# Linear attention, Fourier mixing and a two-layer network in one kernel: the rectifier of the plain groups' second halves moves to one engine, and two pacing numbers behind the folds change

## The chip, the cores and the metric

The kernel runs on one core of a Trainium2 chip. The time is the device time of one execution in microseconds (us); the number that counts is the median of several executions. All arithmetic is in float32.

A core has five engines that run their own instruction queues beside each other: TensorE (PE in the profile) multiplies matrices and transposes, VectorE (DVE) and ScalarE (ACT) work element by element, GpSimd (POOL) does element-wise work and indirect transfers, SyncE (SP) issues most of the other transfers. Each engine takes its instructions in the order in which they stand in its queue, so an instruction that waits holds up all that stand behind it.

## The reference

```
# attention: B=4 batches, H=8 heads, S=768 positions, D=64, decay lam[h] per head
for each block b of 64 positions:
    intra = ((q_b @ k_b^T) * lam^(i-j) for i>=j) @ v_b
    out_b = intra + (q_b * lam^(pos+1)) @ state
    state = lam^64 * state + (k_b * lam^(63-pos))^T @ v_b
x = out, heads side by side                        # [4, 768, 512]
# Fourier mixing and the network
u  = x + real(fft(fft(x, over positions), over channels))
un = (u - mean(u)) / sqrt(var(u) + 1e-6)           # per position
result = u + max(un @ w_ch1, 0) @ w_ch2            # 512 -> 2048 -> 512
```

## The kernel before, in words

**Front and groups.** For each batch b a front runs: the attention (`attn`, six chunks of 128 positions, parts `attn_in` and `attn_out`) and then the Fourier mixing with the normalisation (`fft_ln`). The mixing uses symmetries: rows are added to and subtracted from their mirror images before the transform. These additions are the folds (`fold_a`, `fold_b`, helper `fold_x`), on VectorE. The mirrored rows are first written to DRAM (tiles `xa`, `xb`, by ScalarE's queue, lines 372 to 376) and then gathered back in reverse order by GpSimd (`mirror_a`, `mirror_b`, lines 448 to 461). After the folds come five DFT tiles over the positions (line 525), each copied out by ScalarE (line 529) into `ys`, and then for three tiles t in turn the DFT over the channels (`width`, lines 537 to 542), its combination on VectorE (lines 607 to 611) and the normalisation (`norm`, lines 554 to 585; the power of the variance is taken on GpSimd, line 559).

A batch gives three groups of 256 positions, and the twelve groups are put through the network in two ways. The first four, the list `PLAIN` (batch 0's three groups and batch 1's first), are multiplied directly by `mlp`. The other eight, `LATE`, go in pairs through a recursive product scheme with fewer multiplications (`late`), which needs sums of the weights that `combine_weights` makes on VectorE (line 709). `LATE[-1][0]` is the last batch, 3.

**A plain group.** `mlp(b, g, f0, f1)` takes the hidden channels f0 to f1 in tiles of 128. For each tile four products of 128x128 by 128x256 (line 644; the profile shows each as two instructions) fill a PSUM tile `pm`, of which there are three; the rectified tile goes into `hr`. Then the second layer (line 658) sums over the hidden tiles into PSUM and VectorE adds the result to u (lines 665, 666 or 669, 670). The first three plain groups are run in two calls, hidden tiles 0 to 7 and 8 to 15, the fourth in one call of 0 to 15. In a call that ends at the last hidden tile (`f1 == FO`, FO = 16), the odd tiles are rectified by VectorE (line 650) and the even ones by ScalarE (line 652); in the others all are rectified by ScalarE.

**What sets the order.** All these parts are Python generators. Each yields a number, its declared duration, after it has issued some instructions, and `weave` runs two of them beside each other by these numbers:

```
for d in lead:
    t_lead += d
    while t_other < t_lead * ratio:
        d = next(other, None)
        ...
        t_other += d
```

So the follower is advanced until its declared time has reached the leader's times `ratio`. In the stretch that matters the leader is `fr` (the rest of batch 2's front and batch 3's), the follower `back` (the second halves of the first three plain groups, then the fourth group), and the ratio is (t_back - t_half) / (t_rest - t_rest * t_half / t_back), which comes to t_back / t_rest = 167.6 / 193.6 = 0.8657. A plain step of one hidden tile declares 1.7, a chunk of four second-layer products over 512 columns declares 3.4. In `fft_ln`, lines 513 to 517, the folds of batches 1 to 3 are issued at once (`run`), and a number that is yielded after them makes room for plain work in front of the DFT.

The framework then orders each engine's queue once more: it keeps dependencies, estimates when an instruction could start, and may take a later one first. `keep_in_program_order` pins an instruction behind those that were issued before it; it is used on the first additions of a fold (lines 435, 436) and on the first DFT product of a batch (line 528).

When both fronts are done, the front's memory is released, the first input of the late groups (`ur`) is loaded by ScalarE's queue (`load_u(0, nc.scalar)`, lines 759 and 1233), the first six weight sums are woven with what is left of `back` (line 1234), the last two follow (line 1241), and `late` begins with the sums of line 792 to 798 and the products of line 891.

Of the kernel before, what the change touches and what calls it, by code (L numbers as in the profile page):

```python
# [15 lines left out]
AF = mybir.ActivationFunctionType  # L16
ALU = mybir.AluOpType
# [59 lines left out]
def kernel(  # L77
# [10 lines left out]
    nc = tc.nc  # L88
# [9 lines left out]
    FO = DFF // 128  # L98
# [40 lines left out]
    def new(pool, shape, tag, **kw):  # L139
        cnt[0] += 1  # L140
        return pool.tile(shape, F32, tag=tag, name=f"{tag}{cnt[0]}", **kw)

    def psum_a(shape):
        return new(pa, shape, "pa")

    def psum_m(shape):
        return new(pm, shape, "pm")
# [109 lines left out]
    LEADS = (0,)  # L257
# [207 lines left out]
    def fold_a(b):  # L465
        for a, n in enumerate(BLK):
            yield from fold_x(b, a, n, 1, eo[b][a][1][0:n, 1, 0:DM], xn_[b, HC + a][0:n])

    def fold_b(b, sets):

        tt = nc.vector.tensor_tensor
        for a, n in enumerate(BLK):
            yield from fold_x(b, a, n, 0, xs[b, a][0:n], xs[b, HC + a][0:n])
            e, o = eo[b][a]
            nc.scalar.copy(e[0:n, :, HM:HM + 1], e[0:n, :, DM - 1:DM])

            am, bm = e[0:n, :, W:2 * W], o[0:n, :, W:2 * W]
            lo, hi = e[0:n, 0, 0:HM + 1], e[0:n, 1, 0:HM + 1]
            tt(am[:, 0, 0:HM + 1], lo, hi, op=ALU.add)
            tt(am[:, 1, 0:HM + 1], lo, hi, op=ALU.subtract)  # L480
            yield 0.8

            lo, hi = am[:, :, 0:QM], am[:, :, HM:QM:-1]
            tt(e[0:n, :, 0:QM], lo, hi, op=ALU.add)
            tt(e[0:n, :, QM:HM], lo, hi, op=ALU.subtract)
            yield 0.8
            lo, hi = o[0:n, 0, 1:HM], o[0:n, 1, 1:HM]
            tt(bm[:, 0, 1:HM], lo, hi, op=ALU.subtract)
            tt(bm[:, 1, 1:HM], lo, hi, op=ALU.add)
            yield 0.8  # L490
            lo, hi = bm[:, :, 1:QM + 1], bm[:, :, HM - 1:QM - 1:-1]
            tt(o[0:n, :, 0:QM], lo, hi, op=ALU.subtract)
            tt(o[0:n, :, QM:HM], lo, hi, op=ALU.add)
            yield 0.8
            sets.append((e, o))
        eo.pop(b)
# [3 lines left out]
    def fft_ln(b):  # L500
# [7 lines left out]
        if b in LEADS:  # L508
            yield from fold_a(b)
            yield from fold_b(b, sets)  # L510
            yield 2.0
        else:
            yield 1.0
            run(fold_a(b))
            yield 6.0 if b - 1 in LEADS else 3.0
            run(fold_b(b, sets))
            yield 12.0 if b - 1 in LEADS else 9.0


        for i in range(5):  # L520
            ps = psum_a([128, 2, NK])
# [75 lines left out]
        for t in (1, 2, 0):  # L597
            ps = psum_a([128, DM])
# [14 lines left out]
            if t == 0:  # L613
                ps = psum_a([128, DM])
# [12 lines left out]
    PLAIN, LATE = ORDER[:4], ORDER[4:]  # L627

    def store(b, T, y, cols=slice(0, DM)):
        if T < HC:  # L630
            nc.sync.dma_start(out[b, 128 * T:128 * T + 128, cols], y[:, cols])
        else:
            nc.gpsimd.indirect_dma_start(out=out.rearrange("b s d -> (b s) d"),
                                         out_offset=row_of(2 + HC * (b + 1) + T - HC),
                                         in_=y[:, :], in_offset=None)

    def mlp(b, g, f0=0, f1=FO):

        ut = uts[b, g]
        hr = []  # L640
        for fc in range(f0, f1):
            ps = psum_m([128, G * 128])
            for c in range(KO):
                nc.tensor.matmul(ps, lhsT=w1[:, c, 128 * fc:128 * fc + 128], rhs=ut[:, c, :],  # L644
                                 start=(c == 0), stop=(c == KO - 1))
            if fc % 4 == 0:
                hr.append(new(hp_, [128, 4, G * 128], "hr"))
            t = hr[-1][:, fc % 4, :]
            if fc % 2 and f1 == FO:
                nc.vector.tensor_scalar(t, ps, 0.0, None, op0=ALU.max)  # L650
            else:
                nc.scalar.activation(t, ps, AF.Relu)  # L652
            yield 1.7
        for i in range(G):
            T = TT[g][i]
            ps = psum_m([128, DM])
            for fc in range(f0, f1):
                nc.tensor.matmul(ps, lhsT=hr[(fc - f0) // 4][:, fc % 4, 128 * i:128 * i + 128], rhs=w2[:, fc, :],  # L658
                                 start=(fc == f0), stop=(fc == f1 - 1))
                if fc % 4 == 3 and fc < f1 - 1:  # L660
                    yield 3.4
            u = xs[b, T]
            tt = nc.vector.tensor_tensor
            if f1 < FO:
                tt(u[:, 0:HM], ps[:, 0:HM], u[:, 0:HM], op=ALU.add)
                tt(u[:, HM:DM], ps[:, DM - 1:HM - 1:-1], u[:, HM:DM], op=ALU.add)
            else:
                y = new(up, [128, DM], "y", bufs=1)
                tt(y[:, 0:HM], ps[:, 0:HM], u[:, 0:HM], op=ALU.add)
                tt(y[:, HM:DM], ps[:, HM:DM], u[:, DM - 1:HM - 1:-1], op=ALU.add)  # L670
                store(b, T, y)
            yield 3.4
# [498 lines left out]
    def front(b):  # L1171
        yield from attn(b)
        yield from fft_ln(b)
# [15 lines left out]
    def run(gen):  # L1189
        return sum(gen)  # L1190
# [18 lines left out]
    def beside(lead, t, other, t_other):  # L1209
        return weave(lead, part(other, t_other), t_other / t)  # L1210

    att1, mix = attn(1), fft_ln(0)
    att0 = attn(0)
    run(part(att0, 2.7))
# [3 lines left out]
    run(beside(mix, 24.0, beside(att1, 2.75 * t_chunk, w, 0.16 * NW), 0.16 * NW + 1.75 * t_chunk))  # L1218

    half = [[mlp(b, g, h * FO // 2, (h + 1) * FO // 2) for b, g in PLAIN[:3]] for h in range(2)]  # L1220
    fr = chain([att1, fft_ln(1)] + [front(b) for b in range(2, B)])
    t_rest, t_back = 3 * t_front - 5 * t_chunk, len(PLAIN) * t_mlp - 50.0
    t_half = 1.5 * t_mlp
    run(beside(beside(chain(half[0]), t_half, w, 0.5 * NW), t_half + 0.5 * NW, fr, t_rest * t_half / t_back))
    run(w)
    back = chain(half[1] + [mlp(*PLAIN[3])])
    run(weave(fr, back, (t_back - t_half) / (t_rest - t_rest * t_half / t_back)))
    front_end.close()
# [44 lines left out]
```

## Time and profile before

| | |
|---|---|
| median of the timed executions | 793.8 us |
| each of them | 793.80, 795.42, 793.56 us |
| profiled execution, its own time | 796.12 us |
| its span | 793.9 us |
| mean granted TensorE clock | 0.995 |
| TensorE busy | 763.4 us (96%) |
| VectorE busy | 585.5 us (74%) |
| ScalarE busy | 225.4 us (28%) |
| GpSimd busy | 197.6 us (25%) |
| first-layer products of plain groups, line 644 | 512 instructions |
| rectified by ScalarE, line 652 | 44 x 385 ns = 16.7 us |
| rectified by VectorE, line 650 | 20 x 414 ns = 8.3 us |
| second-layer products of plain groups, line 658 | 256 instructions |

The span is the time from the first to the last event that the profiler recorded. A row of a timeline gives start and duration in us, engine, line, operation, result and operands, the number of instructions run together, and in square brackets the idle time of the engine before it with what ended it. TensorE's rows overlap a little, because matmuls are pipelined and their ends are modelled. A granted clock below 1.00 means that the clock of TensorE was gated for a part of the window.

### The profile page before, as it was taken

Reading aid. Unit: us, or ns where it says so; the run is one execution under the profiler, and the core shown is the slowest. Engines: PE = TensorE matmul, PEld = TensorE weight load, DVE = VectorE, ACT = ScalarE, POOL = GpSimd, SP = SyncE. Lnnn points to the kernel's source line nnn. Section 1 sums busy time; section 2 is a strip of 40 time slices with the busy share of each in tenths; the row PEclk is TensorE's granted clock in tenths of the full one; section 3 lists DMA queues with packets and bytes.
Section 4 is the critical chain, followed back from the end, with each engine's and each line's share of the span. In section 5 each row is a group of like instructions: output and inputs, shape, how many; then the busy total and the mean of one; then the engine's idle time right before and its main releaser. Section 6 shows DMA issues by size and latency. Waiting matters only on the chain.

```text
span 793.9 us, 14617 instructions
## 1 busy us (share of the span) xinstructions
PE 763.4 (96%) x5616; PEld 646.3 (81%) x5616; DVE 585.5 (74%) x1148; ACT 225.4 (28%) x532; POOL 197.6 (25%) x198
## 2 busy tenths in 40 slices
PE   6889989999999999998999999999999999999995
PEld 5768766758585867767946889988999999999995
DVE  6899889675844582345698998769966699758983
ACT  3665443335621221321201221022211342034300
POOL 3223330011111110211004950279205001220021
PEclk9999999999999999999999999999999999999998
DMA  9978723238842147441233374345944455455341
GB/s 243 247 165 245 196 85 129 85 74 205 227 116 77 54 79 146 108 143 64 54 66 107 133 246 162 97 167 191 348 147 153 150 174 185 129 176 186 121 131 70
DMA packets 152331, 116.80 MB, mean 147 GB/s; under 512 B 113998, under 2 KB 113998, under 8 KB 152262
## 3 DMA queue, kind: packets, MB, share of 16 engines
q1 hardware_dynamic: 147120, 103.39, 45.8%
q0 software_dynamic: 2112, 6.69, 2.4%
q10 hardware_dynamic: 3030, 5.78, 2.0%
q8 instruction: 45, 0.74, 0.4%
q14 instruction: 24, 0.20, 0.1%
HBM read 83.58 MB, written 32.25 MB: 146 GB/s over the span
## 4 chain that ended last, share of the span: by engine, by line
PE 78%; DVE 9%; DMA 4%; issue 4%; ACT 1%; POOL 1%; SPq 0%; POOLq 0%; ACTq 0%; DVEq 0%
PE p L1046 21%; PE p L891 12%; PE p L976 11%; PE pm L658 10%; PE pm L644 9%; PE pa L525 3%; PE pa L300 3%; PE pa L341 3%; DMA x<-xb,ix 2%; PE pa L335 2%; PE pa L276 1%; PE pa L357 1%; PE pa L320 1%; DVE sc L304 1%; PE pa L281 1%
## 5 line engine op out<-in xcount | busy, mean ns | idle before, releaser
L644 PE MATMUL pm<-ut,w 128*128 128x256 f32 x512 | 119.7, 384 | 0.0
L658 PE MATMUL pm<-w,hr 128*128 128x512 f32 x256 | 115.7, 596 | 0.2 <-DVE w L227 0.2
L644 PEld LDWEIGHTS pm<-ut,w 128*128 128x128 f32 x512 | 95.6, 192 | 14.2 <-issue 2.1
L658 PEld LDWEIGHTS pm<-w,hr 128*128 128x128 f32 x256 | 46.6, 190 | 49.3 <-issue 48.0
L1060 POOL TENSOR_TENSOR y<-y,u 128x512 f32<-128x512 f32 x12 | 18.8, 1569 | 199.2 <-DVE y L1069 156.8
L1046 PE MATMUL p<-tx,sx 128*128 128x128 f32 x416 | 54.9, 275 | 0.0
L1046 PEld LDWEIGHTS p<-tx,sx 128*128 128x128 f32 x416 | 50.6, 192 | 0.0
L891 PE MATMUL p<-ur,w 128*128 128x256 f32 x192 | 46.9, 379 | 0.1
L272 POOL TENSOR_TENSOR kd<-k,decay 128x512 f32<-128x512 f32 x20 | 22.0, 1100 | 95.3 <-PE pa L320 48.7
L1052 ACT COPY y<-p 128x128 f32<-128x128 f32 x48 | 12.8, 266 | 104.1 <-PE p L1046 103.8
L1054 DVE TENSOR_TENSOR y<-p,y 128x128 f32<-128x128 f32 x92 | 25.5, 286 | 22.5 <-PE p L1046 15.9
L891 PEld LDWEIGHTS p<-ur,w 128*128 128x128 f32 x192 | 36.3, 190 | 5.7 <-issue 0.5
L304 DVE TENSOR_TENSOR sc<-pa,decay 128x512 f32<-128x512 f32 x48 | 31.5, 683 | 8.1 <-PE pa L300 7.9
L1046 PE MATMUL p<-w,ha 128*128 128x128 f32 x288 | 37.4, 275 | 0.0
L300 PEld LDWEIGHTS pa<-qT,kT 64*128 64x128 f32 x384 | 26.1, 193 | 13.4 <-ACT qT L283 7.4
L652 ACT ACTIVATE hr<-pm 128x256 f32<-128x256 f32 x44 | 16.7, 385 | 66.2 <-PE pm L644 66.0
L1046 PEld LDWEIGHTS p<-w,ha 128*128 128x128 f32 x288 | 35.0, 192 | 0.2
L300 PE MATMUL pa<-qT,kT 64*128 64x128 f32 x384 | 30.8, 292 | 3.3 <-ACT qT L283 3.1
L341 PE MATMUL pa<-sc,v 128*64 128x128 f32 x384 | 30.0, 279 | 4.0 <-DVE sc L304 3.8
L558 POOL TENSOR_SCALAR ve<-mv 128x2 f32<-128x2 f32 x12 | 3.4, 286 | 122.3 <-DVE mv L555 122.3
L891 PE MATMUL p<-sx,w1s 128*128 128x256 f32 x128 | 32.9, 380 | 0.2 <-DVE sx L794 0.2
L650 DVE TENSOR_SCALAR hr<-pm 128x256 f32<-128x256 f32 x20 | 8.3, 414 | 32.8 <-PE pm L644 32.8
(234 smaller groups left out, 1736.6 us busy)
## 6 DMA issues: line engine op xcount, KB each, us to landing
tx<-td SPq DMA_DIRECT2D x84, 256.0 KB, 2.7
raw<-in_moe_w_ch_dram SPq DMA_DIRECT2D x32, 512.0 KB, 4.0
tx<-sd SPq DMA_DIRECT2D x42, 256.0 KB, 2.7
sd<-tx SPq DMA_DIRECT2D x28, 256.0 KB, 2.1
k<-in_k_dram SPq DMA_DIRECT2D x24, 256.0 KB, 5.2
q<-in_q_dram SPq DMA_DIRECT2D x24, 256.0 KB, 4.3
v<-in_v_dram SPq DMA_DIRECT2D x24, 256.0 KB, 5.0
td<-tx SPq DMA_DIRECT2D x21, 256.0 KB, 2.0
```

The source lines that it names most:

```text
L272: nc.gpsimd.tensor_tensor(kd, kt, kpow, op=ALU.mult)
L300: mm(pss[hi][:, hp, :], lhsT=kT[HD[hi], hp, :], rhs=qT[HD[hi], hp, :], start=True, stop=True)
L304: nc.vector.tensor_tensor(t, pss[hi], decay[:, hi::2, :], op=ALU.mult)
L341: mm(po[HD[hi], hp, :], lhsT=vt[:, 2 * hp + hi, :], rhs=sc[hi][:, hp, :], start=(c == 0 and hp == 0), stop=(hp == HP - 1), skip_group_chec ...
L525: mm = nc.tensor.matmul(ps[:, n, :], lhsT=piece(a, i, n), rhs=cs[0:rows, a, i in (2, 3), n, :], start=(a == 0), stop=(a == 1))
L644: nc.tensor.matmul(ps, lhsT=w1[:, c, 128 * fc:128 * fc + 128], rhs=ut[:, c, :], start=(c == 0), stop=(c == KO - 1))
L658: nc.tensor.matmul(ps, lhsT=hr[(fc - f0) // 4][:, fc % 4, 128 * i:128 * i + 128], rhs=w2[:, fc, :], start=(fc == f0), stop=(fc == f1 - 1))
L891: nc.tensor.matmul(ps, lhsT=s2.A[a][:, kt, 128 * i:128 * i + 128], rhs=U[b][:, kt, :], start=(first and kt == 0), stop=(kt == 1), skip_gro ...
L976: nc.tensor.matmul(ps[:, 128 * i:128 * i + 128], lhsT=ab[m][0][:, 128 * i:128 * i + 128], rhs=ab[m][1], start=(start and i == 0), stop=Tru ...
L1046: nc.tensor.matmul(ps[:, 0:HM // 2], lhsT=ab[m][0][i], rhs=ab[m][1][:, i, :], start=(start and i == 0), stop=(i == HF // 2 - 1), skip_grou ...
L1054: V.tensor_tensor(o, ps[:, 0:HM // 2], o, op=ADD)
L1060: nc.gpsimd.tensor_tensor(o, y, u, op=ADD)
```

## The change

In `mlp` every tile of the hidden layer is rectified by ScalarE; the branch to VectorE is gone. This concerns 20 tiles: four in each of the three second halves, and eight in the fourth plain group. In `fft_ln` the number that is yielded between the last fold and the first DFT product becomes 10.0 instead of 9.0 for batch 2 and 11.5 instead of 9.0 for batch 3. Batch 1 keeps 12.0, and batch 0 takes another branch. The constants from which the ratio is worked out (`t_front`, `t_rest`, `t_back`) stay as they are.

```diff
@@ fft_ln @@
             run(fold_a(b))
             yield 6.0 if b - 1 in LEADS else 3.0
             run(fold_b(b, sets))
-            yield 12.0 if b - 1 in LEADS else 9.0
+            yield 12.0 if b - 1 in LEADS else 10.0 if b < LATE[-1][0] else 11.5
@@ mlp @@
             t = hr[-1][:, fc % 4, :]
-            if fc % 2 and f1 == FO:
-                nc.vector.tensor_scalar(t, ps, 0.0, None, op0=ALU.max)
-            else:
-                nc.scalar.activation(t, ps, AF.Relu)
+            nc.scalar.activation(t, ps, AF.Relu)
             yield 1.7
```

## The prediction

> **What bounds the kernel now.** I read the busy table first, then the windows of the stretch that the change can reach, then TensorE's and VectorE's timelines there, and last the chain.
>
> ```profile
> PE 763.4 (96%) x5616; PEld 646.3 (81%) x5616; DVE 585.5 (74%) x1148; ACT 225.4 (28%) x532; POOL 197.6 (25%) x198
> ```
>
> TensorE is busy for 96% of the span. The change adds and removes no matmul, so it can only win or lose TensorE's idle time and its slow time. The plain groups' second halves run from about 222 us, and from 428 us TensorE runs full to 781 us. The stakes lie between. In windows of 4 us (columns: length, then TensorE, weight loads, VectorE, ScalarE, GpSimd busy, then granted clock, DMA share, GB/s):
>
> ```profile
> 256.00:260.00 4.00, 3.02 (x15) 2.17 (x14) 3.58 (x11) 0.10 (x1) 0.15 (x1) 1.00 0.00 0
> ...
> 288.00:292.00 4.00, 2.84 (x21) 1.03 (x19) 4.00 (x11) 0.00 (x0) 1.98 (x3) 1.00 0.17 27
> ...
> 362.00:366.00 4.00, 1.96 (x10) 1.43 (x9) 3.74 (x10) 0.20 (x1) 0.00 (x0) 1.00 0.23 66
> 366.00:370.00 4.00, 4.00 (x13) 3.38 (x12) 4.00 (x11) 0.58 (x2) 0.00 (x0) 0.57 0.01 4
> ```
>
> Three holes, at 0.98, 1.23 and 2.04 us, and behind the largest a stretch at reduced clock: in windows of 1 us it is granted 0.56, 0.50, 0.50 and 0.73 from 366 to 370 us, so 0.44 + 0.50 + 0.50 + 0.27 = 1.7 us are lost. TensorE's timeline names what it waits for:
>
> ```profile
> 242.85 13.90 PE L658 MATMUL pm<-w,hr 128*128 128x512 f32 x32
> 257.72 0.90 PE L525 MATMUL pa<-cs,fe 128*128 128x193 f32 x4 [0.98 <-DVE fe L484]
> ...
> 292.07 1.09 PE L341 MATMUL pa<-sc,v 128*64 128x128 f32 x16 [1.23 <-DVE sc L304]
> ...
> 355.66 7.93 PE L644 MATMUL pm<-ut,w 128*128 128x256 f32 x36
> 365.64 0.59 PE L525 MATMUL pa<-cs,fe 128*128 128x193 f32 x2 [2.04 <-DVE fe L484]
> ```
>
> The large hole is batch 3's first DFT product (L525) waiting for the fold on VectorE (L484), after the plain products in front of it (L644) ran out. The chain shows why the fold is late: the gathered rows arrive behind another load.
>
> ```profile
> 353.47 5.60 DMA ur<-utd
> 359.07 0.04 issue
> 359.11 3.13 DMA x<-xb,ix
> ```
>
> Last, VectorE at the end of the stretch. It adds up the weights (L709) without a pause from 401.5 us and then waits for TensorE's last plain product:
>
> ```profile
> 418.90 4.62 DVE L709 TENSOR_TENSOR w<-w 128x1024 f32<-128x1024 f32 x4
> 425.54 0.42 DVE L669 TENSOR_TENSOR y<-pm,x 128x256 f32<-128x256 f32 x1 [2.02 <-PE pm L658]
> ```
>
> So VectorE has 2.02 us of slack there: a gain of TensorE beyond it has to be matched by VectorE.
>
> **Pacing, batch 2 (9 to 10).** One step of plain work is declared as 1.7 and takes TensorE 8 matmul instructions of 3.46/16 = 0.216 us, 1.73 us: units are about microseconds. The code lets plain work run 0.8657 units for each unit of the front (167.6 / 193.6, from its own constants). Counting the declared units from the start of that loop, the front stands at 25.5 at batch 2's first DFT product and plain work at 23.8. One unit more makes 26.5 x 0.8657 = 22.94, still below 23.8, so no step is added in front of that product; the next (3.4 units) only slips from behind the second DFT tile to before it. The trace already has it further ahead: 32 matmuls of L658, four chunks of eight, stand before L525 where the code's order puts three. I cost this edit at nothing; the 0.98 us stay. Bounds: a gain of those 0.98, or a loss of half a chunk, 1.7.
>
> **Pacing, batch 3 (9 to 11.5).** Before, the front's 101.3 units allow 87.7 and four steps lie ahead of the pinned product; with both additions 104.8 allow 90.73, and six steps do (91.8 units). The trace has 36 instructions there, so four and a half steps. After: 48, thus 12 x 0.216 = 2.6 us more. TensorE's plain work then ends at 363.6 + 2.6 = 366.2, not 363.6, and the fold is ready at 365.64: the 2.04 us hole is filled, the product starts 0.55 us late, and the clock should hold. Next late would be the fold's second half. Between the first product and it stand 8 DFT products of 0.165 and 16 plain ones of 0.216, 4.8 us, so TensorE reaches it at 371.0 instead of 372.19; VectorE has it ready (L485) at 370.82, and earlier by the 0.34 of one relu that is gone. So 2.6 us of work more are done 1.2 us sooner: 3.8 us against the profiled execution. Had the clock not dropped, TensorE would have stood there at 370.85 after another short wait, and the gain would be 2.6 - 0.15 = 2.45.
>
> Which of the two counts for the median? The profiled execution took 796.1 us (span 793.9, 2.2 around it). The timed ones took 793.56, 793.80 and 795.42: two agree and the third is 1.7 us above their mean, the size of the clock loss. I read the drop as occurring in some executions, not in the median one, and take 2.45; 3.8 is the far end.
>
> The Trainium skill, "TensorE: Matmul & The Clock Gate", Part 1, says that the clock halves after an idle window of about 3.4 us, and that the window runs free of the program. The drop here follows a hole of only 2.04 us, so the measured row wins on the length; its half rate for some 3.4 us fits, and a free-running window would make it come and go. By its length rule no hole here would cost any clock, and the gain would be 2.45 in every execution.
>
> **20 relus from VectorE to ScalarE.** On VectorE they take 414 ns each, 8.3 us in all; on ScalarE 385 ns, 7.7 us. Neither is a price on the path by itself. On VectorE the slots matter where it is the bound: two relus (286.78 and 290.41 us) lie in the full stretch before the score multiply (L304) of the 1.23 us hole, 0.34 + 0.33 = 0.67 us; I take half, 0.3, because the statistics between them also wait for GpSimd. Four more (385.17, 392.44, 399.01, 399.92) are among batch 3's last norms, about 0.3 each, 1.2 in all; the weight sums start after those norms, so VectorE's end comes forward by 0.6 (where a relu filled a wait of 0.8 to 1.2 us for GpSimd) to 1.2. With the 0.3 this allows TensorE 2.02 + 0.9 to 2.02 + 1.5 = 2.9 to 3.5 us of gain, more than I claim.
>
> On ScalarE each moved relu makes its queue wait for a plain product. What is queued behind: the copies of transposed keys and queries (L278, L283), the state copies (L338), the DFT copies (L529), the fold's column copy (L475) and the store and load issues on its queue. Between 224 and 363 us ScalarE already sits 34.9 us in front of 12 relus, and at 309.7, 313.1, 316.6 and 320.1 us it has 3.07 us free between them, room for one of 0.385: cover is there, and I take zero. The bounds: a gain of the whole 0.67 plus 1.2 on VectorE; a loss of 0.385 to 1.73 + 0.385 = 2.1 us for each copy that is caught behind one.
>
> The skill's "ScalarE: Activation LUTs", Rules for kernel authors, speaks against this edit: relu belongs on VectorE, up to three times faster per element in bf16. This trace's rows are f32 from PSUM, 414 against 385 ns, so it doesn't hold here; by an estimate from that page the moved work would grow to at most 3 x 8.3 = 25 us of ScalarE's time, still beside TensorE.
>
> **Sum.** 2.45 + 0.3 = 2.75 us: 793.8 - 2.75 = 791.05, say 791.0. Against the profiled execution it is 3.8 + 0.3 = 4.1: 796.1 to 792.0. From 428 us on nothing changes but the shift.
>
> **The rivals.**
> - *VectorE's end binds.* If none of the four relus shortens the norms, TensorE gains at most the slack, 2.0 us: 791.8. For it: VectorE is full from 401.5 to 423.5. Against: the relus stand directly between the statistics.
> - *Nothing net.* The framework reorders TensorE's queue by its own estimate of when the fold is ready; its half step ahead of the code's order shows that. If it fills as before, or leaves a new hole of about 2 us elsewhere, 793.8.
> - *ScalarE in the way: slower.* A relu that waits for a plain product stands before a chunk's key and query copies in batch 3's attention, six chunks. At 1.0 us for each, between the 0.385 and 2.1 above, 6.0 us are lost: 791.0 + 6.0 = 797.0. It decides from (2.4 + 2.75) / 6 = 0.86 us a chunk. For it: every second plain step had kept ScalarE's queue free. Against: TensorE has no hole from 296 to 363.6 us, with four such relus inside.
> - *All of it.* The full 4.1, and the 0.98 of batch 2 as well: 788.7.
>
> **How the numbers follow.** Forecast 0.52 (own range 789.7 to 792.0: the gated gain to one of 1.8), VectorE's end 0.12, nothing net 0.10, ScalarE 0.21, all of it 0.05. A measurement tells about 0.3%, 2.4 us, from no change: below 791.4 is faster, above 796.2 slower. Of the forecast's chance 0.42 lies below 791.4. Faster 0.42 + 0.05 = 0.47; same 0.10 + 0.12 + 0.10 = 0.32; slower 0.21. The range runs from 788.5, just under the full gain, to 796.7; ScalarE's case spreads from 795 to 800 and loses some 0.13 above, and 0.04 lies below.
>
> **What would show it.** Right: some 48 plain matmuls before batch 3's first DFT product, its wait on L484 below 0.3 us, clock 1.00 from 366 to 370 us, the hole before L341 at 292 us near 0.9, VectorE's wait before the last L669 cut to under 1 us, and L891 starting 3 to 4 us earlier than in this profile. Wrong: TensorE waits in batch 3's attention released by ScalarE copies (L278, L283, L344); the gather starting later because the load of ur moved on ScalarE's queue; a wait for L709 or L794 in front of L891 above 1 us; or a new hole, with a clock drop, at batch 2's fold.

## The result, and the profile after

The changed kernel takes 798.68 us (median of 19 executions, 795.17 to 804.05) against 794.75 us (19 executions, 793.0 to 798.31) for the kernel before in the same comparison: a ratio of 1.0050, with a 95% interval of 1.0032 to 1.0068. It is slower by 3.9 us, where a gain to 791.0 was forecast and 796.7 was the upper end of the forecast's range.

The profiled execution of the changed kernel took 798.24 us with a span of 796.0. Lines behind 648 have moved up by three: L655 is the former L658, L666 and L667 the former L669 and L670, L706 the former L709, L888 the former L891. The busy table of the page:

```profile
PE 762.9 (96%) x5616; PEld 646.6 (81%) x5616; DVE 578.7 (73%) x1128; ACT 231.4 (29%) x552; POOL 196.6 (25%) x198
```

VectorE lost the 20 relus (585.5 to 578.7 us) and ScalarE took them (225.4 to 231.4). TensorE's work is the same, so the time must lie in its waits. TensorE's timeline of the changed kernel (start, length, line, operands, and in brackets the wait before with its releaser):

```profile
258.11 0.90 PE L525 MATMUL pa<-cs,fe 128*128 128x193 f32 x4 [1.04 <-DVE fe L484]
...
292.72 1.09 PE L341 MATMUL pa<-sc,v 128*64 128x128 f32 x16 [2.04 <-DVE sc L304]
...
356.36 10.52 PE L644 MATMUL pm<-ut,w 128*128 128x256 f32 x48
366.72 0.49 PE L525 MATMUL pa<-cs,fe 128*128 128x193 f32 x2
367.05 1.89 PE L644 MATMUL pm<-ut,w 128*128 128x256 f32 x8
370.96 2.56 PE L525 MATMUL pa<-cs,fe 65*128 65x193 f32 x14 [2.02 <-DVE fe L484]
...
428.21 1.51 PE L888 MATMUL p<-sx,w1s 128*128 128x256 f32 x4 [1.99 <-DVE sx L791]
```

Before, one wait was near 2 us (batch 3's first DFT product) and the others were at 0.98, 1.23 and 0.22. That wait is gone, as forecast: 48 plain instructions now reach to 366.7 us. Three others have taken its place: 2.04 us in front of batch 3's first attention output (1.23 before), 2.02 us in front of the second half of batch 3's fold (the rows with 65 partitions), and 1.99 us where the late groups begin (0.22 before). In this execution the clock held behind the first two and fell behind the third. The windows (last three columns: granted clock, DMA share, GB/s):

```profile
370.00:374.00 4.00, 3.04 (x18) 3.04 (x19) 2.33 (x7) 0.95 (x2) 0.00 (x0) 1.00 0.00 0
...
428.00:432.00 4.00, 3.79 (x10) 3.13 (x11) 1.89 (x5) 0.37 (x1) 2.20 (x4) 0.60 0.17 66
```

What the last wait hangs on stands in the chain of the changed kernel:

```profile
418.88 0.63 DVE e L585
419.53 0.57 SPq L589
...
423.36 2.47 DMA out_dram<-y
425.92 0.42 DVE y L666
426.35 0.39 DVE y L667
426.74 0.61 DVE sx L789
427.37 0.70 DVE sx L791
```

VectorE can't write the fourth plain group's second result (L666 at 425.92) before the first one has been stored, because the tile `y` has one buffer. That store stands on SyncE's queue behind four transfers of the last transposed input (L589), and these wait for the last transpose on VectorE (L585). TensorE had been done with its last plain product at 424.5 us.

### The profile page after: what moved, and what is told of

The parts are those of the page before. It is cut to its first block, busy times and chain, and to the rows that moved or that the text cites. A ratio compares the mean times of both kernels' runs of the same rounds, so it can differ in the third digit from the quotient of the medians.

```text
span 796.0 us, 14616 instructions
## 1 busy us (share of the span) xinstructions
PE 762.9 (96%) x5616; PEld 646.6 (81%) x5616; DVE 578.7 (73%) x1128; ACT 231.4 (29%) x552; POOL 196.6 (25%) x198
## 4 chain that ended last, share of the span: by engine, by line
PE 73%; DVE 13%; DMA 5%; issue 5%; ACT 2%; POOL 1%; SPq 0%; POOLq 0%; ACTq 0%; DVEq 0%
PE p L1043 21%; PE p L888 12%; PE p L973 11%; PE pm L644 7%; PE pm L655 6%; PE pa L341 3%; PE pa L525 3%; PE pa L300 3%; DMA x<-xb,ix 2%; PE pa L335 2%; PE pa L276 1%; DVE stt L554 1%; PE pa L320 1%; DVE un L572 1%; DVE sc L304 1%
## 5 line engine op out<-in xcount | busy, mean ns | idle before, releaser
L644 PE MATMUL pm<-ut,w 128*128 128x256 f32 x512 | 118.1, 381 | 0.0
L655 PE MATMUL pm<-w,hr 128*128 128x512 f32 x256 | 115.7, 596 | 0.0
L655 PEld LDWEIGHTS pm<-w,hr 128*128 128x128 f32 x256 | 46.6, 190 | 49.2 <-issue 48.2
L888 PE MATMUL p<-ur,w 128*128 128x256 f32 x192 | 47.6, 384 | 0.0
L649 ACT ACTIVATE hr<-pm 128x256 f32<-128x256 f32 x64 | 24.2, 384 | 72.8 <-PE pm L644 71.6
L888 PEld LDWEIGHTS p<-ur,w 128*128 128x128 f32 x192 | 37.0, 193 | 5.6 <-issue 0.5
L287 DVE TENSOR_TENSOR qs<-pa,qpow 128x512 f32<-128x512 f32 x20 | 13.7, 686 | 33.2 <-ACT qT L283 33.0
L300 PEld LDWEIGHTS pa<-qT,kT 64*128 64x128 f32 x384 | 26.1, 193 | 13.8 <-ACT qT L283 7.2
L888 PE MATMUL p<-sx,w1s 128*128 128x256 f32 x128 | 33.8, 388 | 2.0 <-DVE sx L791 2.0
L300 PE MATMUL pa<-qT,kT 64*128 64x128 f32 x384 | 30.7, 292 | 3.2 <-ACT qT L283 2.9
L341 PE MATMUL pa<-sc,v 128*64 128x128 f32 x384 | 30.0, 279 | 3.9 <-DVE sc L304 3.8
```

The source lines that it names most:

```text
L300: mm(pss[hi][:, hp, :], lhsT=kT[HD[hi], hp, :], rhs=qT[HD[hi], hp, :], start=True, stop=True)
L341: mm(po[HD[hi], hp, :], lhsT=vt[:, 2 * hp + hi, :], rhs=sc[hi][:, hp, :], start=(c == 0 and hp == 0), stop=(hp == HP - 1), skip_group_chec ...
L888: nc.tensor.matmul(ps, lhsT=s2.A[a][:, kt, 128 * i:128 * i + 128], rhs=U[b][:, kt, :], start=(first and kt == 0), stop=(kt == 1), skip_gro ...
```

## The experiments

Two measures are used throughout. One is taken from one trace each: the time from batch 2's fold to batch 3's fold (both from VectorE's first L435 on gathered rows) and from there to the late groups' first product on `sx`; these leave out the noise of the first 250 us. The other is the mean granted clock over all timed executions of a kernel, each of which has its record: (1 - clock) x span is the clock time that was lost. In the profiled executions 0.9 to 3.0 us of it lies at the idle end of the span, where TensorE has nothing left to do and it costs nothing, so only differences of this number count. The ratios and their intervals are estimated from all executions of a comparison and need not be the quotient of the two medians. For the kernel before, the clocks come from the three comparisons behind the first; e7 has six timed executions, the other runs twelve.

| kernel | ratio to before (95%) | wait before L341, us | waits at batch 3's fold, first and second half | wait at the end of the front | fold 2 to fold 3 | fold 3 to first product on sx | mean clock |
|---|---|---|---|---|---|---|---|
| before | 1 | 1.23 | 2.04, none | 0.22 | 108.0 | 65.5, with a clock drop | 0.9959 to 0.9970 |
| changed | 1.0050 (1.0032 to 1.0068) | 2.04 | none, 2.02 | 1.99 | 108.3 | 65.3 | 0.9940 |
| e1 rectifier only | 0.9983 (0.9963 to 1.0002) | 0.86 | 1.51, none | 0.54 | 107.0 | 64.2 | 0.9962 |
| e9 the same again | 0.9994 (0.9973 to 1.0014) | 0.86 | 2.01, none | 0.54 | 107.4 | 64.2 | 0.9965 |
| e2 both numbers only | 1.0027 (1.0007 to 1.0048) | 1.82 | none, 1.90 | 1.38 | 108.0 | 65.4 | 0.9955 |
| e3 batch 3's number only | 1.0001 (0.9983 to 1.0020) | 1.24 | 1.61, 0.52 | 0.54 | 108.6 | 64.5 | 0.9971 |
| e6 batch 2's number only | 1.0015 (0.9993 to 1.0036) | 1.81 | 1.34, 0.62 | 0.54 | 108.4 | 63.9 | 0.9960 |
| e10 rectifier, batch 2's number | 1.0006 (0.9983 to 1.0028) | 2.05 | 1.33, 0.84 | 0.54 | 110.2, with a drop | 64.1 | 0.9960 |
| e11 rectifier, 13 for batch 3 | 1.0029 (1.0007 to 1.0051) | 0.87 | none, 2.38 | 2.82 | 107.8 | 69.5, with drops | 0.9939 |
| e12 rectifier, 10 for batch 3 | 0.9972 (0.9957 to 0.9988) | 0.86 | 1.37, 0.84 | 0.54 | 107.7 | 64.1 | 0.9978 |
| e7 16 for batch 3 only | 1.0063 (1.0041 to 1.0085) | 1.23 | 0.35 on a relu, none | 5.45 | 108.0 | 68.2, with a drop | 0.9935 |
| e8 rectifier, 16, store moved | 1.0011 (0.9991 to 1.0031) | 0.85 | none, none | 2.86 | 107.0 | 64.5 | 0.9954 |
| e4 changed, store moved | 1.0019 (0.9998 to 1.0039) | 2.05 | none, 2.14 | 1.26 | 110.1, with a drop | 67.9, with a drop | 0.9948 |
| e5 changed again | 1.0051 (1.0028 to 1.0073) | 2.06 | none, 2.25 | 1.98 | 110.3, with a drop | 65.3 | 0.9942 |

### The parts by themselves

**e1: the rectifier only.** The numbers stay at 9 and 9.

```diff
-            if fc % 2 and f1 == FO:
-                nc.vector.tensor_scalar(t, ps, 0.0, None, op0=ALU.max)
-            else:
-                nc.scalar.activation(t, ps, AF.Relu)
+            nc.scalar.activation(t, ps, AF.Relu)
```

> Only the rectifier moves; the pacing numbers stay 9. Theory A (the loss comes from three waits of TensorE of about 2 us, each long enough to halve the clock for some 3.4 us in many executions, and the one at the end of the front is VectorE waiting for the store of the fourth plain group's first result, which stands on SyncE's queue behind the last transposed inputs): the wait before batch 3's first DFT product stays at about 2 us as before, the one before L341 near 292 us is about 2 us instead of 1.2, and the one before the late groups' first product on sx is 1 to 2 us; 2 to 4 us slower than before, 797 to 799. Theory B (the relus on ScalarE's queue hold up copies): TensorE's waits are released by ScalarE copies and are longest in batch 3's attention; also slower, by 4 us or more. Theory C (the extra plain work ahead of batch 3's DFT did it): no slower than before by more than 1 us, 793.5 to 795.5.

Measured 795.74 us against 795.75, a ratio of 0.9983. TensorE's timeline of this kernel:

```profile
290.12 1.09 PE L341 MATMUL pa<-sc,v 128*64 128x128 f32 x16 [0.86 <-DVE sc L304]
364.01 0.59 PE L525 MATMUL pa<-cs,fe 128*128 128x193 f32 x2 [1.51 <-DVE fe L484]
424.81 1.10 PE L888 MATMUL p<-sx,w1s 128*128 128x256 f32 x4 [0.54 <-DVE sx L791]
```

Theories A and B are both wrong here: this part costs nothing that can be measured, and none of TensorE's waits from 200 to 450 us is put down to a ScalarE copy. The wait before L341 even falls from 1.23 to 0.86. What makes that wait 2 us in the changed kernel isn't the rectifier by itself.

**e2: the two numbers only.** Half of the relus stay on VectorE.

```diff
-            yield 12.0 if b - 1 in LEADS else 9.0
+            yield 12.0 if b - 1 in LEADS else 10.0 if b < LATE[-1][0] else 11.5
```

> Only the two pacing numbers, 10 and 11.5; half of the relus stay on VectorE. Theory A: 48 plain matmuls stand before batch 3's first DFT product, so that wait is gone, and one of about 2 us stands before the fold's second half instead; one wait of 2 us as before, so the time is within 1.5 us of before, 793.5 to 796. Theory C: the whole 4 us are here, 797.5 to 799.5. Theory B: the waits behind ScalarE are absent and the filled hole pays: 1.5 to 3 us faster than before.

Measured 797.99 us against 795.75, 1.0027. A loss is here, as theory C said, but only some 2.2 us of the 4. TensorE's timeline shows two of the three waits:

```profile
291.76 1.09 PE L341 MATMUL pa<-sc,v 128*64 128x128 f32 x16 [1.82 <-DVE sc L304]
370.09 2.57 PE L525 MATMUL pa<-cs,fe 65*128 65x193 f32 x14 [1.90 <-DVE fe L484]
```

The two parts don't add up: nothing for the rectifier and 2.2 us for the numbers, but some 4 together. In the traces the three waits are longer with both (2.04, 2.02 and 1.99 us against 1.82, 1.90 and 1.38 + 0.22), and the mean clock is lower (0.9940 against 0.9955, about 1.2 us). Why the clock falls more often there is not shown.

**e3 and e6: one number at a time.**

```diff
# e3
-            yield 12.0 if b - 1 in LEADS else 9.0
+            yield 12.0 if b - 1 in LEADS else 9.0 if b < LATE[-1][0] else 11.5
# e6
-            yield 12.0 if b - 1 in LEADS else 9.0
+            yield 12.0 if b - 1 in LEADS else 10.0 if b < LATE[-1][0] else 9.0
```

> Only batch 3's pacing number, 11.5; batch 2's stays 9. By the declared units plain work stands at 90.1 against 89.86 allowed, so five steps and not six go ahead of batch 3's first DFT product: 40 plain matmuls, and the wait there falls from 2.0 to about 1.2 us; the second half of the fold then waits about 1.2 us too. Theory A: no wait reaches 2 us, the clock holds there in most executions, 1 to 2 us faster than before, 793 to 794. Theory C: half of the loss, 796 to 797.

> Only batch 2's pacing number, 10 instead of 9. Theory D: the wait before L341 near 292 us grows to about 1.8 us, as in the kernel with both numbers, and batch 3's first DFT product finds five plain steps in front of it instead of four and a half; the waits add up to 5.2 to 6 us, 0.5 to 1.5 us slower than before. As my prediction had it, the edit costs nothing: within 0.3 us of before, with 1.2 us near 292 us.

Each of them alone puts five plain steps before batch 3's first DFT product, not six; it takes both to pass the next threshold. e3: 796.11 against 795.75, no difference, where theory A had forecast a gain of 1 to 2 us. e6: 794.17 against 794.11, with 1.0015 (0.9993 to 1.0036) undecided. But the wait before L341 is 1.81 us in e6 and 1.24 in e3: batch 2's number, which I had costed at nothing, lengthens that wait. What this does to the time of the whole kernel e6 alone leaves open.

### With the rectifier moved

After e1 to e8 a new theory, F, was on record: the rectifier wins about 1 us in batch 2's norm, batch 2's number takes it away, and six steps before batch 3's DFT only move the wait. Four runs with the rectifier on ScalarE test it one number at a time.

```diff
# e9: numbers 9 and 9; e10: 10 and 9; e11: 9 and 13; e12: 9 and 10
-            yield 12.0 if b - 1 in LEADS else 10.0 if b < LATE[-1][0] else 11.5
+            yield 12.0 if b - 1 in LEADS else N2 if b < LATE[-1][0] else N3
```

> The rectifier alone on ScalarE, pacing numbers 9 and 9, once more. Theory F (the stretch of batch 2's norm gains about 1 us because relus no longer stand in VectorE's queue before the score multiply; the pacing is what costs): wait before L341 about 0.9, fold of batch 3 to first product on sx about 64.2 us, 0.5 to 2 us faster than before. If the first look was luck: no faster than before, or slower.

> The rectifier on ScalarE and batch 2's number 10, batch 3's 9: five plain steps before batch 3's first DFT product. Theory F: batch 2's number is what makes the wait before L341 about 2 us, 1 us longer from batch 2's fold to batch 3's fold (about 108 instead of 107 us), and the clock is lost behind it in part of the executions; end of the front as with the rectifier alone (64 us). 1 to 2 us slower than the rectifier alone, near before.

> The rectifier on ScalarE, batch 2's number 9, batch 3's 13: six plain steps before batch 3's first DFT product, as in the changed kernel, without batch 2's number. Theory F: wait before L341 about 0.9 us and batch 2's fold to batch 3's 107 us, but the second half of batch 3's fold waits about 2 us, VectorE's weight sums start some 39 us after batch 3's fold instead of 37, and fold to first product on sx takes 65 to 65.5 us: half of the changed kernel's loss, 1 to 2.5 us slower than the rectifier alone.

> The rectifier on ScalarE, batch 2's number 9, batch 3's 10: five plain steps before batch 3's first DFT product. Theory F: wait before L341 about 0.9, at batch 3's fold 1.1 and 0.6 us, weight sums at about 37.5 us after the fold, 63.8 us to the first product on sx: no wait near 2 us, so hardly any clock lost; 1 to 2.5 us faster than before, the fastest of these.

**e9** had 793.95 us against 795.57, the ratio 0.9994 undecided; with e1 the rectifier alone is the same as before or a little faster. Its waits are those of e1.

**e10 against e12** shows how one unit behind batch 2's fold costs at 292 us. Both have five steps before batch 3's DFT product, and from fold 3 on their traces agree to 0.01 us (64.08). TensorE in e12, number 9:

```profile
284.89 1.02 PE L655 MATMUL pm<-w,hr 128*128 128x512 f32 x2
285.84 1.17 PE L300 MATMUL pa<-qT,kT 64*128 64x128 f32 x16
286.94 2.84 PE L655 MATMUL pm<-w,hr 128*128 128x512 f32 x6
...
291.26 1.09 PE L341 MATMUL pa<-sc,v 128*64 128x128 f32 x16 [0.86 <-DVE sc L304]
```

and in e10, number 10:

```profile
284.95 3.60 PE L655 MATMUL pm<-w,hr 128*128 128x512 f32 x8
288.48 1.16 PE L300 MATMUL pa<-qT,kT 64*128 64x128 f32 x16
...
293.36 1.98 PE L341 MATMUL pa<-sc,v 128*64 128x128 f32 x16 [2.05 <-DVE sc L304]
```

In the code's order batch 3's first scores (L300) stood before a chunk of four second-layer products (eight instructions); one unit later they stand behind it. They come 2.6 us later, and VectorE's score multiply loses its place. In e12 it goes between the statistics, at 289.27 and 290.55 us. VectorE's timeline of e10:

```profile
289.66 0.18 DVE L555 BATCH_NORM_AGGREGATE mv<-stt 128x2 f32<-128x6 f32 x1
289.83 0.71 DVE L585 STREAM_TRANSPOSE e<-un 128x512 f32<-128x512 f32 x1
290.58 1.53 DVE L572 TENSOR_SCALAR un<-x,mv,rs 128x256 f32<-128x256 f32 x2
292.03 1.27 DVE L304 TENSOR_TENSOR sc<-pa,decay 128x512 f32<-128x512 f32 x2
```

It stands behind the normalisation (L572, here 1.53 us for two, 0.73 in e12), and TensorE waits 2.05 us instead of 0.86. One of these two took 1.20 us instead of 0.41. This shows only in the traces with both the rectifier on ScalarE and batch 2's number 10 (the changed kernel, e10, e4, e5), where it runs beside GpSimd's product of line 272 (290.90 to 291.96 us in e10). In e6, with the number but not the rectifier, both took 0.41, the product started after them, and the wait was 1.81. That the two engines hinder each other there is my guess; no run tests it. In this execution the clock fell behind that wait as well (0.64 and 0.93 in the windows from 292 to 300 us), so that fold 2 to fold 3 took 110.2 us instead of 107.7. Over all executions e10 has 796.68 us and e12 793.53, and the slowest of e12's twelve (795.06) is faster than the fastest of e10's (795.15).

**e11 against e12** shows the six steps without batch 2's number: 797.74 against 793.53 us. TensorE of e12 at batch 3's fold:

```profile
355.70 8.80 PE L644 MATMUL pm<-ut,w 128*128 128x256 f32 x40
365.87 0.93 PE L525 MATMUL pa<-cs,fe 128*128 128x193 f32 x4 [1.37 <-DVE fe L484]
366.64 1.89 PE L644 MATMUL pm<-ut,w 128*128 128x256 f32 x8
368.37 0.49 PE L525 MATMUL pa<-cs,fo 128*128 128x193 f32 x2
368.69 1.03 PE L644 MATMUL pm<-ut,w 128*128 128x256 f32 x4
370.56 2.23 PE L525 MATMUL pa<-cs,fe 65*128 65x193 f32 x12 [0.84 <-DVE fe L484]
```

and of e11:

```profile
356.39 10.52 PE L644 MATMUL pm<-ut,w 128*128 128x256 f32 x48
366.75 0.55 PE L525 MATMUL pa<-cs,fe 128*128 128x193 f32 x2
367.14 1.89 PE L644 MATMUL pm<-ut,w 128*128 128x256 f32 x8
371.40 4.76 PE L525 MATMUL pa<-cs,fe 65*128 65x193 f32 x14 [2.38 <-DVE fe L484]
```

The second half of the fold is ready some 4.7 us after the first, whatever TensorE does. With five steps the framework fills that time with the other tiles' first halves and 12 plain instructions, and the wait is split into 1.37 and 0.84. With six, it has used the plain work up front, and it goes straight on to the second halves, as if they were ready: 2 DFT products and 8 plain instructions fill 2.2 us, and the rest is a wait of 2.38. The clock then fell to 0.50 and 0.70 in the next two windows of 4 us, which is 3.2 us of clock and most of what the 69.5 us to the first product on `sx` have over the forecast 65 to 65.5.

e12, with the rectifier moved and five steps, is faster than the kernel before: 793.53 us against 795.57, 0.9972 (0.9957 to 0.9988), some 2.2 us by the ratio. Between 240 and 445 us no wait of its trace reaches 1.4 us, and its mean clock over all executions is the highest of all.

### Can enough plain work close both waits?

**e7: 16 for batch 3**, eight steps, the rectifier as before; **e8: the same with the rectifier on ScalarE and the store moved; e4: the changed kernel with the store moved.**

```diff
# e7
-            yield 12.0 if b - 1 in LEADS else 9.0
+            yield 12.0 if b - 1 in LEADS else 9.0 if b < LATE[-1][0] else 16.0
# e8, e4: in store()
-            nc.sync.dma_start(out[b, 128 * T:128 * T + 128, cols], y[:, cols])
+            q = nc.scalar if (b, T) == (1, 1) else nc.sync
+            q.dma_start(out[b, 128 * T:128 * T + 128, cols], y[:, cols])
```

> Only batch 3's pacing number, 16 instead of 9: eight plain steps, 64 matmul instructions, stand before its first DFT product, and the rectifier stays as before. Theory D with a common filler (the plain steps that the changed kernel puts in front of the fold's first wait are the ones that had covered its second): eight steps last until about 370 us and cover both, neither wait is above 0.6 us, and TensorE is some 1.5 us earlier at its last plain product, where it waits for VectorE or the store; waits add up to 4 to 5 us, no clock is lost at batch 3, 0 to 2 us faster than before. If plain work ahead of the DFT delays the front's chain (theory C): slower than the kernel with both numbers, 3 us or more above before.

> The rectifier on ScalarE alone, batch 3's pacing number 16, batch 2's 9, and the store of the fourth plain group's first result from ScalarE's queue. Theory D: waits near 1.0 at batch 2's fold, 0.9 before L341, under 0.6 at batch 3, and 1 to 1.5 us at the end of the front, where VectorE's weight sums end last; 3.5 us in all against 4.65: 1.5 to 3 us faster than before. Theory C: slower than before.

> The changed kernel, with the store of the fourth plain group's first result issued from ScalarE's queue instead of SyncE's; nothing else is touched. Theory A: the store leaves at about 416 us instead of 423.4, VectorE writes the second result as soon as TensorE's last plain product ends, the wait before the late groups' first product on sx falls from 2.0 to under 1 us, and the clock there stays whole: 1.5 to 3 us faster than the changed kernel, about 796 to 797. If that wait doesn't matter: the time of the changed kernel, 798.5 to 799.

e7 closed both waits at batch 3's fold, as expected, and has the highest ratio of all, though its interval overlaps that of the changed kernel: 800.07 us against 794.11. TensorE's timeline:

```profile
370.15 2.90 PE L525 MATMUL pa<-cs,fe 128*128 128x193 f32 x16
...
428.61 2.04 PE L891 MATMUL p<-ur,w 128*128 128x256 f32 x4 [5.45 <-DVE y L670]
```

The waits came back at the end of the front, as one of 5.45 us. VectorE shows the store of `y` in that place:

```profile
427.71 0.42 DVE L669 TENSOR_TENSOR y<-pm,x 128x256 f32<-128x256 f32 x1 [2.13 <-DMA out_dram<-y]
```

e8 was to be 1.5 to 3 us faster than before and was not: 795.36 us against 794.11, the ratio 1.0011 undecided. Though that store leaves from ScalarE's queue there, the wait is still 2.86 us, and VectorE's weight sums end last: 62.1 us after fold 3, against TensorE's last plain product at 59.9. So the end of the front is a race of three: TensorE's plain products, VectorE's weight sums, which start with the last norm and take 22.0 us in every run, and the store. With the rectifier alone TensorE is last (61.9 us after fold 3; weight sums 58.8); in the changed kernel the weight sums end at 61.1 and the store lets VectorE go on at 63.0, TensorE at 61.6. Work taken from TensorE's end and done earlier is a gain only for as long as TensorE is the last of the three.

e4 was to show the store's share: the wait at the end fell from 1.99 to 1.26 us, less than expected, because VectorE's first sum of the late groups (the former L915) moved in between the two sums that TensorE waits for. Its time, 798.54 us against 795.75, is told apart neither from the changed kernel's nor from before's; both other waits are still there, at 2.05 and 2.14 us, each with a clock drop in the profiled execution.

**e5: the changed kernel again.**

> The changed kernel once more, beside the others of this call. Theory D (the time follows the sum of TensorE's waits between 225 and 430 us plus the clock that is lost behind the long ones; before 4.65 us of waits, after 7.29): 2.6 us more for the waits and some 1.5 us for the clock, 3 to 5 us slower than before. Theory E (the first comparison was a matter of its chip): within 2 us of before.

798.78 us against 794.11, 1.0051. The first comparison was no matter of its chip.

## Why the prediction was wrong

*What bounds the kernel.* Right in that TensorE's idle and slow time carry the difference, and that nothing changes behind 430 us but the shift: neither trace has a wait of TensorE of 0.8 us there, and from the first product on `sx` to the end of the span it is 366.1 us before and 367.8 after, where the clock drop at 428 us costs 1.7 (in e9, which has no drop there either, it is 364.8, so these lengths scatter by about 1 us).

*Pacing, batch 2: "I cost this edit at nothing".* This step failed. I checked the one place where the number is yielded, batch 2's first DFT product, and there nothing changed (32 instructions before it, a wait of 1.04 us instead of 0.98). But the unit stays in the leader's sum for all that follows, and some 35 us later it put a chunk of four second-layer products (eight instructions) in front of batch 3's first scores. Beside e12, e10 prices it: a wait of 2.05 instead of 0.86 us, and the clock loss that goes with it in part of the executions.

*Pacing, batch 3: "8 DFT products of 0.165 and 16 plain ones of 0.216".* This step failed too, and with it the forecast gain. The first half came out as worked out (48 instructions, no wait, the product 0.5 us after the fold, 0.55 forecast), and the second half was ready at 370.96 us, 370.82 forecast. But I kept the old filler in front of it. Part of that filler was the very work that had been moved, and the framework took the rest of the order from its own estimate. TensorE found 10 instructions there instead of 24, and waited 2.02 us. Up to the second half it had done 56 plain instructions and 2 DFT products, against 52 and 8 before: 4 x 0.216 us more and 6 x 0.165 less, so nothing was won. The gain of 2.45 us was a wait carried five us on.

*"So VectorE has 2.02 us of slack there".* Mis-read. The slack was that of VectorE, not that of what it waits for next. The store of `y` left at 421.7 us in the trace of before; with the 2.47 us that it took in the trace after, it would have landed at about 424.2, 1.3 us before TensorE's end at 425.5. So by this estimate the slack was 1.3 us, not 2.02. I never asked what stands between VectorE and its next write. The relus themselves did bring the weight sums forward by about what I had said, 0.6 to 1.2 us: with the same numbers they start 39.1 us after fold 3 in the changed kernel against 40.2 in e2, and 36.7 in e10 against 37.6 in e6. But six steps put them back by more: 39.1 against 36.8 with the rectifier alone. In the changed kernel the last transform over the channels (L537) starts 28.7 us after fold 3, in e12 25.5, with 24 plain instructions in front of it instead of 16.

*"the clock should hold".* It fell more often. The mean clock went from 0.9959 to 0.9970 down to 0.9940, which is 1.5 to 2.4 us of the span; three waits near 2 us had taken the place of one. My reading of the timed executions, that the drop comes and goes, was right for before (19 executions reach from 793.0 to 798.3 us, and the clocks recorded later from 0.991 to 0.999).

*The relus.* Right in mechanism and size: 0.3 us was forecast for the wait before L341, 0.37 was measured in e1 (1.23 to 0.86). The rival that ScalarE's queue gets in the way is refuted: with all relus on ScalarE no wait of TensorE that the changed kernel's timeline shows from 200 us on has a ScalarE releaser. The Trainium skill's rule ("ScalarE: Activation LUTs", Rules for kernel authors) that relu belongs on VectorE, with a figure for bf16, didn't hold for these f32 tiles: e1 and e9 are no slower.

*The rivals.* "VectorE's end binds" named the right place but only as a cap on a gain; with the store it is a loss. "Nothing net" named a new wait of 2 us elsewhere as the way to 793.8; there were three.

The sum of what the runs showed, from the changed kernel against e9 (the rectifier alone): 0.9 us from fold 2 to fold 3 (108.3 against 107.4), 1.1 us from fold 3 on (65.3 against 64.2), and 0.0025 x 795 = 2.0 us of clock, 4.0 in all. By the ratios it is (1.0050 - 0.9994) x 795 = 4.5 us.

What stays open: why both parts together cost more than the sum of each; how much of the changed kernel's loss at the end is the store alone, since e4 moved another instruction as well; and batch 2's own wait of 1.0 us, which no run touched.

## What to carry to other kernels

A number that paces two streams acts on everything after it: follow both streams to their end, and look for the places where a short instruction on the path (here a set of score products) changes sides with a long one. Filler is moved, not made: before work is put in front of one wait, ask which later wait it covered, and what ends last where it was taken from. An engine's slack at a wait is that of its whole next step, buffers and stores on other queues included.

## What the runs showed of the hardware

In the fourteen profiled executions there are 15 waits of TensorE of 1.98 us or more between 240 and 445 us. With 10 of them the granted clock went to half, behind the wait or (e7, 5.45 us) within it; with the other 5 it stayed at 1.00, one of 2.86 us among them. With none of the shorter waits in that stretch, up to 1.90 us, did it fall. But 2 us is no threshold: earlier in the span it fell behind a wait of 1.83 us in e3 (at 27 us) and behind two of 1.46 and 0.40 us in e12 (at 68 us), and stayed at 1.00 behind one of 1.87 us in e5 (at 26 us). In windows of 1 us nine of these 12 drops lose 1.7 us each, which at half rate is 3.4 us long, and three lose 3.4 us (one each in e4, e7 and e11). One such drop in the changed kernel, in windows of 1 us:

```profile
428.00:429.00 1.00, 0.79 (x3) 0.77 (x4) 1.00 (x3) 0.00 (x0) 0.28 (x1) 0.88 0.16 61
429.00:430.00 1.00, 1.00 (x4) 0.74 (x3) 0.89 (x3) 0.25 (x1) 0.00 (x0) 0.50 0.53 201
430.00:431.00 1.00, 1.00 (x4) 0.82 (x3) 0.00 (x0) 0.12 (x1) 1.00 (x2) 0.50 0.00 0
431.00:432.00 1.00, 1.00 (x3) 0.80 (x3) 0.00 (x0) 0.00 (x0) 0.92 (x2) 0.50 0.00 0
432.00:433.00 1.00, 1.00 (x6) 0.83 (x5) 0.00 (x0) 0.24 (x1) 0.92 (x2) 0.91 0.00 0
```

The same wait, at the same place and of the same length, drops the clock in one execution and not in another: before L341, 2.04 us left it at 1.00 in the first profile of the changed kernel, and behind 2.06 us it is 0.91 and 0.66 in two windows of 4 us in e5's. Over the changed kernel's 19 executions the time follows the clock: 795.2 us at a mean clock of 0.998, 804.05 at 0.987, and 0.98 us of time for each us of clock lost in a straight line through all of them. They scatter by 2.5 us (standard deviation), those of the kernel before by 1.4 to 2.0 us in the four comparisons, and those of e12 by 0.9. The Trainium skill ("TensorE: Matmul & The Clock Gate", Part 1) gives about 3.4 us of idleness and a window that runs free of the program. Drops of 3.4 us and a free window fit what the traces show, but the drops here follow waits from 1.46 us on.
